# One mask pass instead of two, penalties and signs as steps of the order, a second output buffer, and a new order

## Chip, core, metric

The kernel runs on one core of one Trainium2 chip. The metric is the time of one execution in microseconds (us), the median of three runs. The engines are TensorE (PE, matrix products), VectorE (DVE), ScalarE (ACT), GpSimd (POOL) and SyncE (SP, which here issues the transfers).

## What is computed

Local attention with a few global keys, followed by one dense feed-forward layer. With 4 batches, 8 heads, 768 positions, head size 64, `n_global` 8 and `n_local` 96:

```python
scores = scale * np.matmul(q, k.transpose(0, 1, 3, 2))
keep = is_global | is_local                  # pos < n_global, or 0 <= rel < n_local
bias = -slopes[:, None, None] * dist         # dist: rel, or n_local for a global key that isn't local
scores = np.where(keep, scores + bias, -1e9)
a = softmax(scores); x = np.matmul(a, v)     # 3072 rows of 512
h = x @ w_in                                 # 512 x 2048
sp = np.maximum(h, 0.0) + np.log1p(np.exp(-np.abs(h)))
out = (h * erf(sp)) @ w_out                  # 2048 x 512
```

`q`, `k`, `v` are float32; `w_in` and `w_out` reach the kernel as float64.

## The kernel before

**Tiles.** The 3072 rows are 24 tiles of 128 (six to a batch). A tile's queries meet 256 columns: 120 keys of the tile before, 8 global keys, 128 keys of its own. Two tiles make a unit of 256 rows for the feed-forward part, whose 2048 inner columns are two groups of 1024, each in two halves of 512. Matrix products of the feed-forward part are made in float16 with each operand split into a high and a low half, three products for one.

**Order.** All work of the fast path is a list of steps, `ORDER`, written out as a table. Each word is a step's name, its numbers and, where the engine can be chosen, a letter: `a` ScalarE, `v` VectorE, `p` POOL. `run_fast` calls the steps in that order, and every engine executes its own instructions in the order in which they were recorded. Since one helper records everything, nearly all instructions have the line L195. The names that matter here:

- `Wd`, `Rd`: a transfer of weights. `w_in` comes in eight blocks of 1 MB (`w_in_raw`, into the tile `wo`, four buffers, each used again once its block is done), `w_out` in sixteen chunks of 512 KB (`wo_load`, twelve in tiles named `raw_wo` and four in `wo`).
- The turn from float64 to float32, on the two 32-bit words of each number, in place: `Wi`/`Ri` scales the high word as a float32 (`conv_i`), `Wa`/`Ra` shifts the low word right (`conv_a`; on ScalarE it moves 16-bit halves instead), `Wc`/`Rc` puts the sign into the upper half of the low word (`conv_c`), `Wb`/`Rb` joins the two (`conv_b`). The words stand 8 bytes apart from one element to the next.
- `Wq`, `Wr`, `Wm`, `Wp` and the same with R: a gram product, its maximum, a sum over partitions, and power-of-two scales; then `Wh`/`Rh` and `Wl`/`Rl` make the high and the low float16 half.
- `vd`, `vq`, `vm`, `vp`: the same scales for `v`. `ld` loads a tile of k, q or v; `TK`, `K`, `KC`, `KF` turn k and copy it into the key buffer `kT`, `TQ` and `Qc` do q.
- `S` scores (PE), `E` adds the penalty `pen` and takes the minimum (a custom DVE instruction), `X` exp (ACT), `eh`, `el`, `et` (`eP` for the first tiles) the float16 halves of e and their transpose, `V` the product with v, `x`, `xh`, `xl`, `xt` the attention output.
- `h` up projection (PE) and `H` its copy out of PSUM; `t`, `l`, `i`, `G` tanh, logs, exp and gelu on ScalarE; `P`, `Q`, `c`, `C` products; `g`, `j` the float16 halves; `d` down projection (PE, tile `o`); `O` the scaled output tile (`osb`) and `o` its store.

**Setup.** `setup` reads the two counts, builds a flag that chooses the fast path, issues the first transfers and calls `fast_masks`. That function runs a chain of DVE instructions on a buffer (in `wi_lo`) twice: in the first pass for the first tile of a batch, in the second for the others. After the first pass ScalarE writes two of three column blocks of the penalty for each of 8 heads, 16 instructions; after the second POOL writes the third, 8 instructions. All of it stands ahead of the branch to the fast path on these engines.

Of the kernel before, what the change touches and what calls it, by code (L numbers as in the profile page):

```python
# [74 lines left out]
vh1a Wa3v Wc3 X1,2,1 S2,0 eh1,0,0a ld3,0 Wm2 eh1,0,1a X1,2,0 Ra0a Wb3 V0,2 Wh1a el1,0,1 E2,0,1 vl1 Wp2 Rd5 Wd4 Wq3 va1
Wi4a eP1,2,0 Wr3a x0 eh1,2,0a Wl1 Ri5p Wa4v E2,0,0 X2,0,0 Rc2 Rd3 Wc4 Wd5 Wb4 X2,0,1 el1,0,0 vq1,0,6 Rd1 eP1,2,1
eh1,2,1a Ri4p el1,2,0 Wh2v Ra5a el1,2,1 Wm3 Wi5a vd1,1,6 Wq4 ld2,2 Wl2 S2,2 Wr4a xP0 Wp3 V1,0 Rd6 Wh3a eh2,0,1v V1,2
TK3 Rc0 E2,2,1 eh2,0,0v Ra1a x1 xh0a Wa5a Wl3 el2,0,1p K3a xP1 va2 Wd7 xl0v xh1v X2,2,1 Ra4a Wm4 Wp4 Rc5 xl1v ld3,1
Ri1v Ri3a Wc5 et2,0,1 Rc4 vh2p Ri6p h0,0 Wd6 Rb2 Rc1 Ra6a E2,2,0 Wi7a Rb1 Ra3v Wb5 el2,0,0v Rb0 TQ3 Qc3a ld4,0 Wa7v
h0,1 Wc7 H0,0a Wb7 X2,2,0 eh2,2,1a Rd7 Wh4a Wq5 S3,0 vq1,1,6 Ri7p et2,0,0 Rd12 Wl4 el2,2,1v Rb4 Rd13 Rc3 Wi6a Rc6  # L80
H0,1v h0,2 Wr5v Wa6a Wm5 vl2 et2,2,1 Rb3 eh2,2,0a Wc6 E3,0,1 Ra7a h0,3 E3,0,0 Wp5 TK4 Rq0 vd1,2,6 Ri13v Wb6 Rd14 Wh5a
Rb5 Rc7 Rr0a X3,0,1 Rb6 S3,2 el2,2,0p H0,2a Wl5 Ri12p eh3,0,1v V2,0 vq1,2,6 Wq6 Wq7 el3,0,1p Rd15 E3,2,0 et2,2,0 Ri15p
X3,0,0 Wr6v Rd8 Ra13a X3,2,0 ld3,2 E3,2,1 Wr7a X3,2,1 Rb7 Ri14a Rd10 et3,0,1 Rc13 h1,0 Wm6 Rd9 Ri8p Ra15a K4a Ra12v
Rb13 Ra14v eh3,0,0a Wp6 V2,2 Wm7 x2 Ra8v Wh6p xh2a Wl6 vh3a H1,0a Ri10a Wp7 Wh7a ld4,1 eh3,2,0a Ra10v Rm0 H0,3a Rq1
Rd11 vl3 Rr1a el3,0,0v Rp0 Rc12 vd1,3,6 Rc15 Ri9a Rc10 Rb12 Rc8 Rb10 ld4,2 h1,1 TQ4 Rc14 Ra9a et3,0,0 Rb15 Rc9 Qc4a
h1,2 t0,0 Rb14 vq1,3,6 xl2p ld5,0 S4,0 Ri11a Rq3 TK5 Rb9 ld5,1 Ra11a Rm1 Rr3a va3 Wl7 Rm3 Rh1a eh3,2,1v ld6,0 Rh2a Rb8
el3,2,0p Rp1 H1,1a Rc11 Rh0v Rb11 Rq2 Rl1 K5a et3,2,0 Rh3a Rp3 vd1,4,6 Rr2a H1,2a E4,0,0 vh4a Rl0 t0,1 Rm2 el3,2,1p
Rp2 E4,0,1 t1,0 vq1,4,6 S4,2 Rh11a et3,2,1 Rh10v vl4 Rh8p V3,0 V3,2 Rl10 Rh4p h1,3 xt2 Rl8 TQ5 x3 Rl4 xh3v X4,0,0 l0,0
Rl2 Rh13p eh4,0,0a X4,0,1 xl3v vd1,5,6 Rl11 Rh6p Qc5a vq1,5,6 Rh5p Rh9p E4,2,0 el4,0,0v i0,0 Rh7v E4,2,1 eh4,0,1a xt3
ld6,1 H1,3v Rl6 vm1 el4,0,1v X4,2,1 Rl5 Rl13 G0,0 vd2,0,6 Rl9 X4,2,0 Rl7 h2,0 h2,1 P0,0v vp1 et4,0,0 H2,0a et4,0,1  # L90
eh4,2,0v l0,1 S5,0 Rh12p Q0,0p TK6 G0,1 eh4,2,1v E5,0,0 va4 h2,2 X5,0,0 el4,2,0p et4,2,0 c0,0 E5,0,1 H2,1v Rl12 C0,0
ld7,0 H2,2a g0,0v S5,2 el4,2,1p K6a X5,0,1 h2,3 V4,0 j0,0 E5,2,1 Rl3 TQ6 ld5,2 i0,1 eh5,0,0v l1,0 P0,1v X5,2,1 h3,0
vh5p el5,0,0p et4,2,1 Qc6v eh5,0,1v E5,2,0 i1,0 va5 H2,3v vq2,0,6 d0,0 d0,1 el5,0,1p d0,2 t2,0 Rh14p t1,1 Q0,1v vl5
et5,0,0 KC1,0p G1,0 c0,1 C0,1 h3,1 S6,0 et5,0,1 eh5,2,1a V4,2 E6,0,0 X5,2,0 x4 vd2,1,6 el5,2,1p E6,0,1 ld7,1 d0,3 V5,0
# [1100 lines left out]
```

## Time and profile before

| | |
|---|---|
| median of three runs | 723.23 us (722.84 to 723.86) |
| the profiled execution | 723.82 us; its span, first to last instruction, 722.0 us |
| TensorE busy, mean granted clock | 660.6 us (91%), 0.969 |
| VectorE, ScalarE, POOL busy | 615.2 us, 629.9 us, 233.7 us |

The profile is one execution on the core. Busy time of an engine is a mean over stages with different limits, so a stage's own window tells more than the share of the span. A matmul's end is modelled.

### The profile page before, as it was taken

What the parts mean: (1) busy time and instruction counts of PE and PEld (TensorE: products, weight loads), DVE (VectorE), ACT (ScalarE), POOL (GpSimd) and SP (SyncE); (2) the same over time, 40 slices, a digit from 0 to 9 for tenths busy, and PEclk for the clock granted to TensorE, in tenths of its full rate; (3) what the DMA queues carried; (4) which work ended last, traced back from release to release, by engine and by line L of the source; (5) the groups of instructions that cost most, each with busy time, mean ns of one, the idle gap of its engine ahead of it and who ended that gap; (6) DMA issues with size and microseconds to landing.
All of it is one profiled execution on the core that took longest, in us unless ns stands there. A gap on an engine that the chain in (4) does not pass through costs nothing.

```text
span 722.0 us, 14148 instructions
## 1 busy us (share of the span) xinstructions
PE 660.6 (91%) x5384; PEld 458.9 (64%) x5384; DVE 615.2 (85%) x1141; ACT 629.9 (87%) x1001; POOL 233.7 (32%) x174
## 2 busy tenths in 40 slices
PE   2864768889999999999999999999999999999995
PEld 1553657666675677666766766666776766667552
DVE  3899998899999978998878898999958789867682
ACT  4577778999999999899999999789899999998970
POOL 2031121356342244123642136121533421624200
PEclk9987987799999999999999999999999999999998
DMA  8675986545656655556436565356454454230000
GB/s 264 187 234 171 277 253 112 122 90 117 132 136 115 133 103 118 120 94 110 103 85 129 96 132 116 64 85 127 95 104 114 92 104 88 40 63 30 1 31 34
DMA packets 207553, 83.40 MB, mean 116 GB/s; under 512 B 192988, under 2 KB 192988, under 8 KB 207476
## 3 DMA queue, kind: packets, MB, share of 16 engines
q1 hardware_dynamic: 207476, 82.41, 51.6%
q8 instruction: 44, 0.72, 0.4%
q14 instruction: 33, 0.27, 0.1%
HBM read 41.96 MB, written 6.29 MB: 67 GB/s over the span
## 4 chain that ended last, share of the span: by engine, by line
PE 75%; DVE 16%; ACT 4%; issue 2%; DMA 2%; POOL 1%; POOLq 0%; SPq 0%; DVEq 0%; ACTq 0%
PE h L195 30%; PE o L195 30%; PE s L195 7%; PE po L195 4%; DVE wo L195 3%; DVE e L195 2%; PE kTp L195 1%; PE qTp L195 1%; DVE C L195 1%; DVE raw_wo L195 1%; DVE g L195 1%; DVE wi_lo L195 1%; DVE w L195 1%; DMA kraw<-in_k 1%; ACT L195 1%
## 5 line engine op out<-in xcount | busy, mean ns | idle before, releaser
L195 PE MATMUL h<-xT,wi_hi 128*128 128x256 f16 x1536 | 260.3, 275 | 5.0 <-DVE ex_wi L195 1.6
L195 PE MATMUL o<-wo,g 128*128 128x512 f16 x1152 | 262.7, 379 | 0.1
L195 PE MATMUL h<-xT,wi_lo 128*128 128x256 f16 x768 | 211.2, 275 | 0.0
L195 PEld LDWEIGHTS <-g 128*128 128x128 f16 x1152 | 110.2, 98 | 123.7 <-issue 5.9
L195 PEld LDWEIGHTS <-wi_hi 128*128 128x128 f16 x1536 | 149.4, 99 | 33.1 <-issue 5.4
L195 ACT ACT_TABLE_LOAD x100 | 128.3, 1283 | 1.8
L195 POOL TENSOR_TENSOR w<-e,w 128x512 f16<-128x512 f32 x44 | 63.8, 1451 | 146.8 <-DVE w L195 86.7
L195 ACT ACTIVATE e<-e,mn 128x256 f32<-128x256 f32 x192 | 95.3, 498 | 14.6 <-DVE mn L195 14.2
L195 PEld LDWEIGHTS <-wi_lo 128*128 128x128 f16 x768 | 75.8, 99 | 11.3 <-issue 1.8
L195 DVE SCALAR_TENSOR_TENSOR C<-A,B 128x1024 f32<-128x1024 f32 x48 | 64.6, 1346 | 10.6 <-POOL B L195 10.3
L195 DVE SCALAR_TENSOR_TENSOR g<-C,gs,g 128x1024 f16<-128x1024 f32 x48 | 65.2, 1358 | 8.5 <-POOL g L195 8.0
L195 PE MATMUL s<-kT,qT 64*128 64x256 f32 x384 | 63.2, 437 | 6.0 <-DVE mn L195 3.6
L195 DVE CUSTOM_DVE_ANT_0 e<-s,pen 128x256 f32<-128x256 f32 x160 | 60.5, 418 | 9.4 <-PE s L195 7.6
L195 POOL TENSOR_SCALAR g<-C,gs 128x1024 f16<-128x1024 f32 x24 | 33.3, 1387 | 107.3 <-DVE C L195 81.5
L195 DVE SCALAR_TENSOR_TENSOR C<-C,H 128x1024 f32<-128x1024 f32 x48 | 62.1, 1294 | 0.6
L195 ACT ACTIVATE B<-A 128x1024 f32<-128x1024 f32 x48 | 50.8, 1057 | 5.7 <-DVE C L195 2.9
L195 ACT ACTIVATE A<-A,halves 128x1024 f32<-128x1024 f32 x48 | 54.8, 1142 | 0.2
L195 POOL TENSOR_TENSOR B<-C,B 128x1024 f32<-128x1024 f32 x17 | 41.6, 2447 | 38.7 <-DVE A L195 30.2
L195 PEld LDWEIGHTS s<-kT,qT 64*128 64x128 f32 x384 | 37.3, 202 | 23.4 <-issue 11.8
L195 ACT ACTIVATE C<-A 128x1024 f32<-128x1024 f32 x48 | 50.4, 1053 | 1.0 <-DVE g L195 0.6
L195 ACT ACTIVATE B<-B 128x1024 f32<-128x1024 f32 x48 | 50.2, 1050 | 0.3
L195 ACT ACTIVATE A<-H 128x1024 f32<-128x1024 f32 x48 | 50.0, 1050 | 0.2
(153 smaller groups left out, 974.5 us busy)
## 6 DMA issues: line engine op xcount, KB each, us to landing
wo<-in_moe_w_in SPq DMA_DIRECT2D x8, 1024.0 KB, 9.2
raw_wo<-in_moe_w_out SPq DMA_DIRECT2D x12, 512.0 KB, 6.8
out<-osb SPq DMA_DIRECT2D x24, 256.0 KB, 2.8
qraw<-in_q SPq DMA_DIRECT2D x23, 256.0 KB, 3.6
kraw<-in_k SPq DMA_DIRECT2D x23, 256.0 KB, 3.3
vraw<-in_v SPq DMA_DIRECT2D x23, 256.0 KB, 3.8
va<-vb SPq DMA_DIRECT2D x20, 240.0 KB, 3.6
vm<-in_v SPq DMA_DIRECT2D x18, 256.0 KB, 5.9
```

Source lines behind the costliest of these rows:

```text
L195: i = getattr(self.engine, name)(*a, **k)
```

## The change

What it does:

1. `fast_masks` runs one chain for both kinds of tile and leaves three column blocks (`pd`) side by side: block 0 for the previous keys of a batch's first tile, block 1 for those of the others, block 2 for a tile's own. The global columns get their two forms by three small instructions.
2. The penalty of one head is one instruction of 128x384, a step `pn` of the order with an engine letter. Eight such steps replace the 24 instructions of setup: four on POOL, three on DVE, one on ScalarE.
3. The sign step is a copy of the high word into a float16 (after `conv_i` the number is so small that only its sign is left), with an engine letter. Of 24, ScalarE has 17 (6 `Wc`, 11 `Rc`), POOL 6 (2 and 4), DVE 1.
4. Setup's flag takes fewer DVE instructions; POOL's clearing of the global v rows comes after the mask work.
5. The very last output tile has a buffer of its own (tag `x`), and `osb` is kept for each tile.
6. `ORDER` is another permutation of the same steps, with other letters. Over the whole list, 53 of the float16 copies of e are on ScalarE (41 before), 52 of 88 differences `el` on POOL (44), 46 copies `H` on ScalarE (53).

```diff
-Wi0a TK0 vd0,1,3 K0a TQ0 Qc0a KC0,0p S0,0 E0,0,1 ld1,1 ld1,0 Wa0v Wd1 X0,0,1 TK1 Wc0 vd0,0,3 vd0,2,3 eP0,0,1 K1a
+TK0 K0a Wi0v pn3p pn5v pn6v vd0,1,3 pn2p vq0,1,3 TQ0 Wa0v Qc0a KC0,0p vd0,2,3 pn1p Wc0p ld0,2 S0,0 vd0,0,3 ld1,0
...
-d23,7 O11,0a o11,0 O11,1a o11,1
+d23,0 d23,1 c23,1 d23,2 C23,1 d23,3 g23,1v j23,1 d23,4 d23,5 d23,6 d23,7 O11,0a o11,0 O11,1v o11,1
...
-    def conv_c(self, r):
-
-        s = r.bitcast(I16).rearrange("p a (b w) -> p a b w", w=4)[:, :, :, 1]
-        self.nc.vector.tensor_scalar(s, self.words(r)[1], 0.0, -32768.0, op0=ALU.is_lt, op1=ALU.mult)
+    def conv_c(self, r, e):
+        s = r.bitcast(F16).rearrange("p a (b w) -> p a b w", w=4)[:, :, :, 1]
+        if e == "a":
+            self.nc.scalar.copy(s, self.words(r)[1])
+        else:
+            (self.nc.vector if e == "v" else self.nc.gpsimd).tensor_copy(s, self.words(r)[1])
...
-        for c in range(2):
-            act, pd = mk[:, 2], mk[:, 3]
...
-            for h in range(H):
-                s = -8.0 * SLOPES[h]
-                if c == 0:
-                    nc.scalar.activation(self.pen[:, h, 0], pd[:, 0:P], AF.Copy, scale=s)
-                    nc.scalar.activation(self.pen[:, h, 2], pd[:, P:], AF.Copy, scale=s)
-                else:
-                    nc.gpsimd.tensor_scalar(self.pen[:, h, 1], pd[:, 0:P], s, 1.0, op0=ALU.mult, op1=ALU.mult)
+        nc.gpsimd.memset(pd[:, 0, 0:PREV], big)
...
+        v = nc.vector
+        v.tensor_scalar(act, rel, nl, None, op0=ALU.is_lt)
+        v.scalar_tensor_tensor(act, rel, 0.0, act, op0=ALU.is_ge, op1=ALU.mult)
+        v.tensor_scalar(gl, jg, ng, None, op0=ALU.is_lt)
+        v.tensor_scalar(act[:, g], act[:, g], -1.0, 1.0, op0=ALU.mult, op1=ALU.add)
+        v.tensor_tensor(act[:, g], act[:, g], gl, op=ALU.mult)
+        v.tensor_tensor(rel, act, rel, op=ALU.mult)
+        v.tensor_scalar(rel[:, g], act[:, g], nl, None, op0=ALU.mult)
+        v.tensor_scalar(act, act, -big, big, op0=ALU.mult, op1=ALU.add)
+        two = lambda z: z.rearrange("p (k w) -> p k w", k=2)
+        v.tensor_tensor(pd[:, 1:3], two(rel), two(act), op=ALU.add)
+        v.tensor_copy(pd[:, 0, g], pd[:, 1, g])
+        v.tensor_scalar(gb, gl, -big, big, op0=ALU.mult, op1=ALU.add)
+        v.scalar_tensor_tensor(pd[:, 1, g], gl, nl, gb, op0=ALU.mult, op1=ALU.add)
+        self.pd = pd
+
+    def penalty(self, h, z):
+        s, o = -8.0 * SLOPES[h], self.pen[:, h]
+        if z == "a":
+            self.nc.scalar.activation(o, self.pd, AF.Copy, scale=s)
+        elif z == "v":
+            self.nc.vector.tensor_scalar(o, self.pd, s, None, op0=ALU.mult)
+        else:
+            self.nc.gpsimd.tensor_scalar(o, self.pd, s, 1.0, op0=ALU.mult, op1=ALU.mult)
...
-        o = self.xp.tile([P, DM], F32, tag="osb", name=f"osb_{u}_{t}")
+        tag = "x" if u == B * NT // UT - 1 and t else "osb"
+        o = self.xp.tile([P, DM], F32, tag=tag, name=f"osb_{u}_{t}")
```

The table's rows say little to a reader, so here is where the instructions stand. First DVE behind the branch to the fast path, before the change: `e` and `mn` are a custom instruction (printed as ISA) that makes a masked tile and its minimum, `wo` is the first block of `w_in`, shifted and joined.

```order
L195 ISA e_0_1_216,mn_205<-s_0_1_211,pen 128x256
L195 ISA mn_205 128x1
L195 TENSOR_SCALAR wo<-wo 128x1024 x2
L195 ISA e_0_0_244,mn_205<-s_0_0_210,pen 128x256
L195 ISA mn_205 128x1
L195 ISA e_0_0_244,mn_205<-s_0_0_210,pen 128x256
L195 ISA mn_205 128x1
L195 SCALAR_TENSOR_TENSOR wo<-wo 128x1024
```

Both minima of the first head pair stand ahead of the joining there. The same place on DVE after the change:

```order
L195 TENSOR_SCALAR wo<-wo 128x1024
L195 TENSOR_SCALAR pen<-wi_lo 128x384 x2
L195 TENSOR_SCALAR wo<-wo 128x1024
L195 SCALAR_TENSOR_TENSOR wo<-wo 128x1024
L195 TENSOR_SCALAR pen<-wi_lo 128x384
L195 ISA e_0_1_209,mn_177<-s_0_1_189,pen 128x256
L195 ISA mn_177 128x1
```

The scaling of the first block, two penalties, the shift, the joining and a third penalty now stand ahead of the first minimum; the sign step between shift and joining is gone from DVE.

POOL at the start, before: `pen` are the penalties, `kT` the key buffer (a clearing, then two copies).

```order
L654 TENSOR_SCALAR pen<-wi_lo 128x128 x8
L1156 TENSOR_LOAD flag
L1157 COMPARE_AND_BRANCH
L195 MEMSET kT 128x4x120
L195 TENSOR_SCALAR kT<-kT 128x4x2x8
L195 TENSOR_SCALAR kT<-kT 128x4x8
L195 TENSOR_SCALAR vb_336<-wo,s_v_326 128x8x64
```

All eight penalties, and the branch, are ahead of the key buffer there. POOL at the start after the change:

```order
L195 MEMSET kT 128x4x120
L195 TENSOR_SCALAR pen<-wi_lo 128x384 x2
L195 TENSOR_SCALAR kT<-kT 128x4x2x8
L195 TENSOR_SCALAR pen<-wi_lo 128x384
L195 CAST wo<-wo 128x1024
L195 TENSOR_SCALAR pen<-wi_lo 128x384
L195 TENSOR_SCALAR kT<-kT 128x4x8
L195 TENSOR_SCALAR raw_wo_202<-raw_wo_202 128x512
```

Two of four larger penalties stand ahead of the copy of the keys where eight small ones stood, and the sign of the first block (CAST of `wo`) between the third and the fourth.

Third, DVE in the stage in which the chunks of `w_out` are turned, before: of the rows on `raw_wo`, the TENSOR_SCALAR ones are shifts and signs, the SCALAR_TENSOR_TENSOR ones join.

```order
L195 TENSOR_SCALAR raw_wo_420<-raw_wo_420 128x512
L195 TENSOR_SCALAR wo<-wo 128x1024
L195 TENSOR_SCALAR raw_wo_466<-raw_wo_466 128x512
L195 SCALAR_TENSOR_TENSOR raw_wo_427<-raw_wo_427 128x512
L195 TENSOR_SCALAR raw_wo_420<-raw_wo_420 128x512
L195 ISA e_2_0_784,mn_473<-s_2_0_624,pen 128x256
L195 ISA mn_473 128x1
L195 ISA e_2_0_784,mn_473<-s_2_0_624,pen 128x256
L195 ISA mn_473 128x1
L195 SCALAR_TENSOR_TENSOR raw_wo_420<-raw_wo_420 128x512
L195 TENSOR_SCALAR raw_wo_427<-raw_wo_427 128x512
```

Shifts, signs and joinings of three chunks alternate there. The same stage on DVE after the change (`wi_lo` is a low half of `w_in`, `vb` the v of a tile):

```order
L195 SCALAR_TENSOR_TENSOR wi_lo<-wo,swi,wi_hi 128x4x256
L195 SCALAR_TENSOR_TENSOR raw_wo_202<-raw_wo_202 128x512
L195 SCALAR_TENSOR_TENSOR raw_wo_676<-raw_wo_676 128x512
L195 SCALAR_TENSOR_TENSOR vb_687<-vraw_2_659,s_v_298,vb_687 128x8x64
L195 SCALAR_TENSOR_TENSOR raw_wo_387<-raw_wo_387 128x512
L195 TENSOR_SCALAR wo<-wo 128x1024
L195 SCALAR_TENSOR_TENSOR raw_wo_473<-raw_wo_473 128x512
L195 TENSOR_SCALAR wo<-wo 128x1024
```

On DVE the joinings of four chunks now follow one another, without a sign between them. The signs (CAST of `raw_wo` and of `wo`) stand in this part of ScalarE's queue, where `e` are exps, `gr_wi` a gram maximum, `vm` a square of v and `H` a copy out of PSUM:

```order
L195 ACTIVATE e_2_1_590,sm_476<-e_2_1_590,mn_475 128x256 x2
L195 CAST raw_wo_262<-raw_wo_262 128x512
L195 CAST wo<-wo 128x1024
L195 ACTIVATE raw_wo_473<-raw_wo_473 128x512
L195 ACTIVATE raw_wo_202<-raw_wo_202 128x512
L195 CAST raw_wo_202<-raw_wo_202 128x512 x2
L195 ACTIVATE gr_wi_757,a_wi_808<-gr_wi_757 128x256
L195 ACTIVATE vm_1_385,a_v_374<-vm_1_385 128x512
L195 CAST raw_wo_473<-raw_wo_473 128x512
L195 ACTIVATE H_0_791<-h_1_766,hs_301 128x512
```

Five signs came into these ten rows, among ScalarE's own scalings of chunks.

## Rows read from the trace of the kernel before

**Rows 1.** The page, part 2: busy tenths of TensorE and VectorE in 40 slices
```profile
PE   2864768889999999999999999999999999999995
...
DVE  3899998899999978998878898999958789867682
```

**Rows 2.** Windows: busy us (instructions) of each engine, granted clock, DMA share
```profile
160.00:300.00 140.00, 139.89 (x1161) 94.21 (x1159) 132.18 (x237) 134.84 (x224) 56.52 (x38) 1.00 0.58 119
...
0.00:20.00 20.00, 5.62 (x22) 3.62 (x22) 7.71 (x36) 8.87 (x25) 4.83 (x22) 1.00 0.89 263
20.00:160.00 140.00, 102.74 (x855) 82.19 (x854) 131.04 (x317) 108.47 (x207) 35.16 (x31) 0.85 0.71 183
...
153.70:713.45 559.75, 557.94 (x4583) 378.75 (x4583) 482.60 (x803) 516.04 (x778) 195.79 (x123) 1.00 0.47 95
```

**Rows 3.** Waits of DVE, 20 to 160 us: total, times, longest
```profile
DVE x L195 <- PE po L195: 2.1, 1, 2.1
```

**Rows 4.** The chain that ended last: start, us, what
```profile
160.28 3.89 PE o L195 x18
```

**Rows 5.** Groups by form, DVE, 0 to 160 us: busy us, mean ns, idle before
```profile
L195 DVE TENSOR_SCALAR wo<-wo 128x1024 int16<-128x1024 f32 x8 | 11.0, 1369 | 0.3
...
L195 DVE TENSOR_SCALAR raw_wo<-raw_wo 128x512 int16<-128x512 f32 x12 | 9.3, 811 | 0.0
...
L195 DVE TENSOR_SCALAR wo<-wo 128x512 int16<-128x512 f32 x4 | 3.1, 782 | 0.0
```

**Rows 6.** Timeline 0 to 40 us: start, us, engine, instruction, [idle before]
```profile
2.12 0.58 SPq L269 DMA_DIRECT2D wo<-in_q  x1
...
11.40 1.10 ACT L195 ACTIVATE wo<-wo 128x1024 f32<-128x1024 f32 x1
11.53 0.43 DVE L641 TENSOR_TENSOR wi_lo<-wi_lo 128x256 f32<-128x256 f32 x1 [2.11 <-ACT pen L652]
...
13.11 2.42 POOL L654 TENSOR_SCALAR pen<-wi_lo 128x128 bf16<-128x128 f32 x8 [10.82 <-DVE wi_lo L645]
...
16.34 2.08 PE L195 MATMUL s<-kT,qT 64*128 64x256 f32 x8 [2.20 <-POOL kT L195]
...
18.58 0.42 DVE L195 CUSTOM_DVE_ANT_1 e<-s,pen 128x256 f32<-128x256 f32 x1 [5.57 <-PE s L195]
```

**Rows 7.** Groups by form, DVE, whole span
```profile
L195 DVE TENSOR_SCALAR hs<-iwi,s_v 128x8 f32<-128x8 f32 x3 | 4.5, 1499 | 0.1
...
L195 DVE TENSOR_SCALAR hs<-iwi,s_v 128x1 f32<-128x1 f32 x8 | 1.7, 214 | 0.3
...
L644 DVE TENSOR_SCALAR wi_lo<-wi_lo 128x256 f32<-128x256 f32 x2 | 0.6, 294 | 0.1
```

**Rows 8.** Groups by form, POOL, whole span
```profile
L654 POOL TENSOR_SCALAR pen<-wi_lo 128x128 bf16<-128x128 f32 x8 | 2.2, 297 | 11.0 <-DVE wi_lo L645 10.8
L195 POOL TENSOR_SCALAR wo<-wo 128x1024 f32<-128x1024 f32 x1 | 1.8, 1779 | 4.4 <-DMA wo<-in_moe_w_in 4.4
...
L195 POOL TENSOR_SCALAR wi_hi<-wo,swi 128x1024 f16<-128x1024 f32 x1 | 1.2, 1170 | 2.9 <-DVE iwi L195 2.9
```

**Rows 9.** Groups by form, ACT, whole span
```profile
L195 ACT ACTIVATE raw_wo<-raw_wo 128x512 int16<-128x512 uint16 x9 | 12.2, 1357 | 0.0
...
L195 ACT ACTIVATE wo<-wo 128x1024 int16<-128x1024 uint16 x3 | 7.5, 2510 | 0.0
...
L195 ACT ACTIVATE wi_hi<-wo,swi 128x1024 f16<-128x1024 f32 x6 | 7.4, 1239 | 4.8 <-DVE swi L195 4.8
...
L195 ACT ACTIVATE wo<-wo 128x1024 f32<-128x1024 f32 x5 | 5.8, 1158 | 1.5 <-DMA wo<-in_moe_w_in 1.5
...
L195 ACT ACTIVATE raw_wo<-raw_wo 128x512 f32<-128x512 f32 x3 | 2.2, 722 | 0.0
```

**Rows 10.** Timeline 705 to 723 us
```profile
713.47 0.69 ACT L195 ACTIVATE osb<-o,gs 128x512 f32<-128x512 f32 x1 [11.52 <-PE o L195]
...
716.63 0.69 ACT L195 ACTIVATE osb<-o,gs 128x512 f32<-128x512 f32 x1 [2.47 <-DMA out<-osb]
```

More of the change, by code (lines that the diff above doesn't have):

```diff
@@ L75 @@
[L75 to L94, printed above, removed]
@@ new lines @@
+eh4,2,1v P0,0v et4,0,0 H1,3a E5,0,1 X4,2,0 l0,1 el4,2,1p eh4,2,0v E5,0,0 va4 Q0,0v et4,2,1 h2,1 vh4a TK6 H2,0a
+el4,2,0v S5,2 vl4 G0,1 Rh12p H2,1a c0,0 vd2,0,6 et4,2,0 Rl9 t1,0 X5,0,0 ld5,2 h2,2 h2,3 V4,0 C0,0 Rl12 K6a eh5,0,0a
+ld7,0 V4,2 g0,0v X5,0,1 i0,1 TQ6 eh5,0,1a Rh13v H2,2v E5,2,1 j0,0 el5,0,0p et5,0,0 h3,0 el5,0,1p l1,0 Qc6v H2,3v P0,1v
+E5,2,0 vh5a d0,0 X5,2,1 vl5 KC1,0p d0,1 Q0,1v G1,0 h3,1 Rl13 d0,2 t2,0 va5 c0,1 S6,0 t1,1 eh5,2,1a ld7,1 X5,2,0 x4
+C0,1 E6,0,0 et5,0,1 d0,3 i1,0 H3,0v TQ7 X6,0,0 el5,2,1p V5,0 E6,0,1 xh4a g0,1p eh5,2,0v S6,2 ld6,2 el5,2,0v P1,0v
@@ new lines @@
+et5,2,1 h3,3 Qc7a H3,1a TK7 X6,0,1 j0,1 ld8,1 d0,4 eh6,0,0a l1,1 E6,2,0 KC1,1p Q1,0v K7v X6,2,0 Rh14a xl4p c1,0
+et5,2,0 h3,2 d0,5 C1,0 xt4 vq2,0,6 i1,1 Rl14 V5,2 eh6,2,0a x5 el6,0,0p E6,2,1 et6,0,0 g1,0v vd2,1,6 l2,0 TQ8 d0,6 xh5v
+eh6,0,1a j1,0 H3,2v d0,7 G1,1 vq2,1,6 xl5v vh6p S7,0 d1,0 d1,1 el6,2,0p et6,2,0 xt5 vl6 G2,0 P1,1v Rh15v ld8,0
+el6,0,1p E7,0,1 E7,0,0 t2,1 H3,3v Rl15 X6,2,1 Q1,1p c1,1 C1,1 et6,0,1 i2,0 eh6,2,1a d1,2 g1,1v l2,1 ld9,1 d1,3 S7,2
+h4,2 X7,0,1 i2,1 h4,0 t3,0 vd2,2,6 j1,1 d1,4 P2,0v d1,5 G2,1 Qc8v d1,6 el6,2,1v Q2,0v va6 eh7,0,1v vq2,2,6 c2,0 d1,7
@@ new lines @@
+C15,0 eh19,2,1a g15,0p S20,0 H16,3a P15,1p E20,0,0 el19,2,1v X19,2,0 h17,0 ld21,1 E20,0,1 Q15,1p ld21,0 l16,0 d14,3
+eh19,2,0v xh18a h17,2 H17,0a c15,1 TQ21 X20,0,0 j15,0 d14,4 C15,1 S20,2 X20,0,1 d14,5 el19,2,0p Qc21a V19,0 g15,1p
+h17,1 E20,2,0 TK21 ld20,2 xl18v et19,2,1 et19,2,0 d14,6 V19,2 X20,2,0 xt18 G16,0 d14,7 K21a vh20a eh20,0,0a H17,1a
+ld22,1 j15,1 t16,1 el20,0,0p d15,0 H17,2v i16,0 x19 xh19v xl19v d15,1 vl20 o6,1 E20,2,1 l16,1 d15,2 P16,0v S21,0
+et20,0,0 eh20,0,1a i16,1 xt19 d15,3 el20,0,1v eh20,2,0a d15,4 E21,0,0 X20,2,1 Q16,0p G16,1 el20,2,0v P16,1p h17,3
@@ L184 @@
+d21,7 h23,3 O10,0a h23,2 P22,1p o10,0 Q22,1v j22,0 c22,1 G23,0 O10,1a H23,2a d22,0 d22,1 H23,3v o10,1 C22,1 P23,0v
+g22,1v j22,1 t23,1 l23,1 Q23,0v c23,0 i23,1 d22,2 G23,1 d22,3 C23,0 d22,4 d22,5 g23,0v d22,6 j23,0 P23,1v Q23,1v d22,7
+d23,0 d23,1 c23,1 d23,2 C23,1 d23,3 g23,1v j23,1 d23,4 d23,5 d23,6 d23,7 O11,0a o11,0 O11,1v o11,1
 """.split()]
@@ L234, in setup @@
         lo, hi = f2[:, 0, :], f2[:, 1, :]
-        neg = cp.tile([P, 2], F32, name="nneg")
-        nc.vector.tensor_scalar(neg, lo, 0.0, None, op0=ALU.is_lt)
         hi2 = cp.tile([P, 2], F32, name="nhi2")
-        nc.vector.tensor_tensor(hi2, hi, neg, op=ALU.add)
+        nc.vector.scalar_tensor_tensor(hi2, lo, 0.0, hi, op0=ALU.is_lt, op1=ALU.add)
         self.nval = cp.tile([P, 2], F32, name="nval")
@@ L617, in fast_masks @@
         self.pen = cp.tile([P, H, 3, P], BF16, name="pen")
-        mk = self.wi_lo.rearrange("p c f -> p (c f)").bitcast(F32)[:, 0 : 4 * WIN].rearrange("p (a w) -> p a w", a=4)
-        rel, jg, gl = mk[:, 0], mk[:, 1, 0:NGL], mk[:, 1, NGL : 2 * NGL]
+        big = BIG / SLOPES[-1]
+        mk = self.wi_lo.rearrange("p c f -> p (c f)").bitcast(F32)
+        rel, act = mk[:, 0:WIN], mk[:, WIN : 2 * WIN]
+        pd = mk[:, 2 * WIN : 2 * WIN + 3 * P].rearrange("p (k w) -> p k w", k=3)
+        jg, gl, gb = (mk[:, 4 * WIN + k * NGL : 4 * WIN + (k + 1) * NGL] for k in range(3))
         it = lambda o, n, base: nc.gpsimd.iota(
@@ L974, in o_part @@
             self.nc.vector.tensor_scalar(o, po, s, None, op0=ALU.mult)
-        self.osb = o
+        self.osb[u, t] = o
     def o_store(self, u, t):
         r = u * U + t * P
-        self.nc.sync.dma_start(self.out[r : r + P, :], self.osb)
+        self.nc.sync.dma_start(self.out[r : r + P, :], self.osb.pop((u, t)))
     def gen_batch(self, b):
@@ L1060, in branch @@
             self.cb, self.hb = (CB, HB) if fast else (1, 2)
-            for n in ("pt", "vs", "qT", "us", "vm", "a_v", "gr", "a1", "hs", "h_done", "raw_wo", "raws", "tp", "cs", "va", "vb", "xT", "hp", "H", "A", "B", "C", "g", "pos"):
+            for n in ("pt", "vs", "qT", "us", "vm", "a_v", "gr", "a1", "hs", "h_done", "raw_wo", "raws", "tp", "cs", "va", "vb", "xT", "hp", "H", "A", "B", "C", "g", "pos", "osb"):
                 setattr(self, n, {})
@@ L1090, in run_fast @@
         do = dict(
-            Wd=self.w_in_raw,
+            pn=self.penalty, Wd=self.w_in_raw,
             Wi=lambda n, z: conv(lambda r: self.conv_i(r, z), self.wi_raw(n)),
             Wa=lambda n, z: conv(lambda r: self.conv_a(r, z), self.wi_raw(n)),
-            Wc=lambda n: conv(self.conv_c, self.wi_raw(n)),
+            Wc=lambda n, z: conv(lambda r: self.conv_c(r, z), self.wi_raw(n)),
             Wb=lambda n: conv(self.conv_b, self.wi_raw(n)),
```

221 lines of the change are left out of this document (104 added, 117 removed).

## The prediction

> **What bounds the kernel now.** I read the page first, then the windows by stage. The page shows where TensorE lacks work: its row of tenths starts with nine digits from 2 to 8 and is then 9 up to the last slice, while the row of VectorE (DVE) is 8 and 9 from the second slice on [rows 1]. The windows show it in numbers. From 20 to 160 us DVE is busy 131.04 of 140 us, ScalarE (ACT) 108.47, and TensorE 102.74 at a granted clock of 0.85; from 153.70 to 713.45 us TensorE is busy 557.94 of 559.75 at 1.00 [rows 2]. So the program has two parts. In the first the weights are turned from float64 into two float16 halves and the first tiles of attention are made; DVE sets its pace. DVE's longest wait between 20 and 160 us is one of 2.1 us [rows 3]; five shorter ones follow it in that view. It waits for hardly anybody. The second part begins about the first down projection, at 160.28 us [rows 4], and TensorE sets its pace to the end. TensorE's work is the same in both kernels (the order holds the same matmul steps), so the end moves by as much as the first down projection moves, plus what the last output saves, plus stalls that a new order may put into the second part.
>
> **What is removed from DVE.** The sign step runs 24 times on DVE: 8 instructions of 11.0 us, 12 of 9.3 and 4 of 3.1, 23.4 us, all before 160 us [rows 5]. In the new order one of the 24 stays on DVE as a cast (at most the 0.78 of the old form, and not below zero). The second mask pass goes: in the timeline its end releases POOL's penalties at 13.11, and DVE is idle 2.11 us inside it because ScalarE's penalties still read the buffer [rows 6]; its eight instructions are the same as in the first pass, 2.5 us of work.
>
> **What is added to DVE before the first down projection.** Three penalties of 128x384, a form that the trace does not show. The nearest row is the 128x256 multiply-add at 294 ns [rows 7]; by its size one is 0.44, all three 1.3. Bounds for one are 0.29 and 0.88 (three times that of 128x128 on POOL, 297 ns, [rows 8]), so 0.9 to 2.6. Four more shifts of the low words (5 to 6 and 5 to 8 by the letters, 0.4 to 0.7 each, estimated as a half of the sign step) give 2.0, and one more maximum of a gram of w_in and two of w_out about 1.8. The attention steps that change engines before that point nearly cancel (two fewer float16 copies of e, two more copies of q, one product, one v scaling): +0.3. Sum: 23.4 + 2.5 - 0.8 - 1.3 - 2.0 - 1.8 - 0.3, near 20 us; durations overlap by some 50 ns at each start, so I take **18 us less DVE**.
>
> **What ScalarE pays.** It gets 6 signs of 128x1024 and 11 of 128x512, f32 in and f16 out, at a step of 8 bytes. The trace has no such form. Two rows lie on either side: the float32 scaling in place at the same step takes 1158 and 722 ns, and the 16-bit shift in place, also at that step, 2510 and 1357 [rows 9]. By the first the signs cost 6 x 1.158 + 11 x 0.722 = 14.9 us, by the second 6 x 2.510 + 11 x 1.357 = 30.0. I take the first: the input is 32 bits wide as there, and the writing of float16 from a stepped float32 (the high half of w_in) also took only 1239 [rows 9]. ScalarE sheds 16 penalties (their starts stand 0.2 apart, 3.2 us), four 16-bit shifts (2.5 + 3 x 1.36 = 6.6), two halves of w_in (2.5) and two scalings of w_in (2.3), and gets two scalings of w_out (1.4) and one penalty of 128x384 (0.3 to 0.9). With the maxima that leave it, that is about 0 to +2: **ScalarE's work up to the first down projection stays near the 117.3 us of the trace** (8.87 and 108.47, [rows 2]).
>
> [...]
>
> **The start.** Before, the first scores wait for POOL's copies of k, which stand behind eight penalties of 2.42 us in POOL's queue; DVE idles 5.57 us and its first mask-and-minimum begins at 18.58 [rows 6]. In the new order DVE reaches the branch when one mask pass is done (about 8.5 us), and then waits for w_in's first block, which had landed by 11.40, when ScalarE used it [rows 6]. Behind that wait stand two penalties, the shift, the sign on POOL (1.17 to 1.78, [rows 8]) and the combining step, so the scores' first minimum comes at about 17, and the first block of w_in is ready five to six us sooner. DVE has thus done about 12 us of work by 20 us, where it had done 7.71 [rows 2].
>
> **First down projection.** DVE's work up to 160 us was 7.71 + 131.04 = 138.75 [rows 2]; less 18 it is 120.7. With 12 done at 20 us, 108.7 remain. Were DVE as dense as before (0.936), they would take 116 us and the projection would come at 136. But ScalarE now has as much to do (117 less some 9), and each waits for the other on every block of weights. From 160 to 300 us the two are busy 0.94 and 0.96 together [rows 2], so two full engines are possible; I choose 0.86, since here a chain of eight blocks with four buffers runs through both. 108.7/0.86 = 126, so it comes at 146: **14 us sooner**. Bounds: 0.936 gives 24 sooner, 0.76 gives 3.
>
> **The last output.** The second tile of the last output waits 2.47 us for the store of the first, from one buffer, and starts at 716.63, 3.16 after the first [rows 10]. With a buffer of its own and on DVE it starts with the first at 713.47; its store queues behind the first store's issue (0.58 for as many bytes, [rows 6]). **2.5 us saved**; 0 if the store's issue were the limit, 3.2 at most.
>
> **Stalls later.** From 160 to 300 us ScalarE has 5.2 us of 140 free [rows 2]. In that part the new order gives it about 4 us more than before (five more float16 copies of e, one more log step, fewer copies out of PSUM), and over the whole rest about 1. I charge 1.5 (0 to 6).
>
> **Sum.** 723.82 (the profiled execution, span 722.0 and 1.8 around it) - 14 - 2.5 + 1.5 = 708.8. The median is 0.6 below the profiled execution, so **708 us**. Under 0.2% (1.4 us) a change of this kernel can't be told from none.
>
> **The rivals.**
> 1. *Forecast*, 703 to 713 us: chance 0.60. A density over 0.90 would give less than 703: 0.06.
> 2. *The sign copy costs ScalarE what its 16-bit shift costs.* Then it has 15 us more, some 132 up to the first down projection; at 0.86 behind the first 20 us that is 163, no gain, and only the last output and the start remain: 718 to 722. For it: the 16-bit row at the same step. Against: the float32 input, and that the shift also converts integers. 0.13. [...]
> 3. *POOL takes from DVE what the change gives.* POOL has about 11 us more before the first down projection (two more scalings and halves of w_in each, six signs). The row that shows the two colliding is a product of 128x8 on DVE, 1499 ns on average in three, where one of 128x1 takes 214 [rows 7]. If each of those 11 us held DVE up, 3 of the 14 were left: 718 to 719. Against: DVE was 0.94 busy beside POOL anyway, and much of DVE's work there reads PSUM. 0.06. [...]
> 4. *The weights don't come sooner.* The DMA engines are busy 0.71 of 20 to 160 us [rows 2]; the same bytes in 126 us need 0.79, and 0.89 was reached in the first 20. If the queue adds half of the saving back: 715 to 716. 0.08.
> 5. *Slower.* ScalarE passes work that it could not do into the second part. There it has 43.7 us free of 559.75, but only 5.2 up to 300 us, so a backlog of B us stalls TensorE by up to B. It decides from B = 16.5 on, where 14 + 2.5 are eaten: 725 and more. For it: 11 signs at the end of the weights, just before the first tanh and log groups. Against: they are 0.7 us each, and ScalarE had 31 us of idle time between 20 and 160. 0.07.
>
> The range must leave out no more than 0.2: from 702 to 719 it holds case 1, case 4, most of case 3 and the near half of the 0.06 on one side and of case 2 on the other. Faster: cases 1, 3, 4, the 0.06 and nearly all of 2, 0.90. Same: the end of case 2 and between 2 and 5, 0.03. Slower: 0.07.
>
> **What would show it.** Right: no 16-bit multiply on DVE; ScalarE's casts at 1.1 to 1.3 us for 1024 and about 0.7 for 512; the first minimum at about 17 us; the first down projection near 146; both engines at 0.85 or so from 20 us to there; two output tiles starting together at the end. Wrong: casts over 2 us, DVE instructions that stretch while POOL is busy, TensorE idle by more than 3 us after the first down projection.

## The result, and the profile after

| | before | after |
|---|---|---|
| median | 723.55 us (722.84 to 724.44, 4 runs) | 714.29 us (713.80 to 714.79, 4 runs) |
| profiled execution, span | 723.82 us, 722.0 us | 713.80 us, 711.6 us |

The ratio is 0.987, 95% interval 0.985 to 0.989: the change saves 9.3 us. Forecast were 708 us and a range of 702 to 719; the time lies in the range, and the gain is 9 us where 15 were expected.

The page of the changed kernel, part 2, has TensorE's tenths a little higher at the start than in [rows 1], and VectorE no longer at 9 there:

```profile
PE   3668777999999999999999999999999999999996
...
DVE  5788788999999979898897799888977999795894
```

The windows of the changed kernel, with the columns of [rows 2]. The first `o` matmul starts at 153.8 and the last output at 705.04, so the window of 551.24 us is the second part:

```profile
0.00:20.00 20.00, 7.82 (x36) 5.97 (x36) 10.69 (x36) 9.93 (x20) 9.12 (x21) 1.00 0.91 270
20.00:160.00 140.00, 109.49 (x906) 87.28 (x906) 120.50 (x305) 126.03 (x210) 44.64 (x36) 0.79 0.74 189
160.00:300.00 140.00, 140.00 (x1175) 96.00 (x1173) 131.51 (x234) 136.25 (x233) 68.35 (x41) 1.00 0.60 119
...
0.00:153.80 153.80, 111.11 (x900) 89.25 (x901) 124.99 (x329) 129.83 (x221) 51.73 (x56) 0.81 0.76 199
153.80:705.04 551.24, 550.87 (x4484) 372.79 (x4483) 478.48 (x775) 510.38 (x775) 213.81 (x129) 1.00 0.47 95
```

Read against the window of before: from 20 to 160 us VectorE fell from 131.04 to 120.50, but ScalarE rose from 108.47 to 126.03. I read this as one engine that set the pace before and two that share it now; runs 2, 3, 5 and 10 test it. The waits of VectorE from 20 to 160 us say the same (total, times, longest); in [rows 3] the longest was one of 2.1 us for TensorE:

```profile
DVE wo L195 <- ACT wo L195: 6.5, 4, 2.7
DVE e L195 <- PE s L195: 3.5, 2, 2.3
DVE raw_wo L195 <- ACT raw_wo L195: 1.9, 1, 1.9
DVE raw_wo L195 <- POOL raw_wo L195: 1.2, 1, 1.2
```

The rows for `wo` and `raw_wo` are VectorE's joinings, waiting for signs. The groups by form name the reason (busy us, mean ns, idle before); they answer to [rows 5] and stand beside the shift of [rows 9]:

```profile
L195 ACT CAST wo<-wo 128x1024 f16<-128x1024 f32 x6 | 15.8, 2640 | 1.7 <-issue 1.7
L195 ACT CAST raw_wo<-raw_wo 128x512 f16<-128x512 f32 x8 | 11.2, 1484 | 0.0
L195 ACT ACTIVATE raw_wo<-raw_wo 128x512 int16<-128x512 uint16 x7 | 10.3, 1476 | 0.0
L195 POOL CAST raw_wo<-raw_wo 128x512 f16<-128x512 f32 x4 | 6.9, 1731 | 11.5 <-ACT raw_wo L195 9.2 <-DVE raw_wo L195 2.3
L195 POOL CAST wo<-wo 128x1024 f16<-128x1024 f32 x2 | 4.9, 2473 | 4.5 <-ACT wo L195 3.6 <-DVE wo L195 0.9
...
L195 ACT CAST wo<-wo 128x512 f16<-128x512 f32 x3 | 4.3, 1428 | 0.0
```

A sign copy costs ScalarE 2640 and 1484 ns, the price of the 16-bit shift in the same trace (2598 and 1476) and not that of the float32 scaling (1206 and 762). The 17 took 31.3 us (15.8 + 11.2 + 4.3) where 14.9 were reckoned.

The start, to set beside [rows 6]:

```profile
9.19 0.93 DVE L195 TENSOR_SCALAR wo<-wo 128x1024 f32<-128x1024 f32 x1 [0.79 <-DMA wo<-in_moe_w_in]
...
11.67 2.47 POOL L195 CAST wo<-wo 128x1024 f16<-128x1024 f32 x1 [0.88 <-DVE wo L195]
...
14.17 1.23 DVE L195 SCALAR_TENSOR_TENSOR wo<-wo 128x1024 int32<-128x1024 int32 x1 [2.57 <-POOL wo L195]
...
15.90 0.41 DVE L195 CUSTOM_DVE_ANT_1 e<-s,pen 128x256 f32<-128x256 f32 x1
```

The first minimum comes at 15.90 (18.58 before), although VectorE waits 2.57 us for POOL's copy of 2.47. And the end, beside [rows 10]:

```profile
705.04 0.69 ACT L195 ACTIVATE osb<-o,gs 128x512 f32<-128x512 f32 x1 [11.51 <-PE o L195]
705.68 0.75 DVE L195 TENSOR_SCALAR osb<-o,gs 128x512 f32<-128x512 f32 x1 [5.02 <-PE o L195]
705.75 1.56 SPq L195 DMA_DIRECT2D out<-osb  x2
```

The second tile starts 0.64 behind the first instead of 3.16, and both stores go out together. From 705.04 to the end of the span are 6.6 us; before, from 713.47, 8.5.

So the 10.4 us between the spans of these two executions split into three: 6.3 because the first down projection starts at 153.8 instead of 160.1, 2.1 because the second part is 551.2 long instead of 553.4, and 1.9 at the end.

### The profile page after: what moved, and what is told of

The parts are those of the page before. It is cut to its first block, busy times and chain, and to the rows that moved or that the text cites. A ratio compares the mean times of both kernels' runs of the same rounds, so it can differ in the third digit from the quotient of the medians.

```text
span 711.6 us, 14143 instructions
## 1 busy us (share of the span) xinstructions
PE 662.6 (93%) x5384; PEld 462.1 (65%) x5384; DVE 604.2 (85%) x1104; ACT 640.9 (90%) x995; POOL 265.5 (37%) x184
## 5 line engine op out<-in xcount | busy, mean ns | idle before, releaser
L195 POOL TENSOR_TENSOR w<-e,w 128x512 f16<-128x512 f32 x52 | 74.3, 1432 | 133.9 <-ACT w L195 68.8
L195 PE MATMUL s<-kT,qT 64*128 64x256 f32 x384 | 65.3, 448 | 8.7 <-DVE mn L195 4.8
L195 DVE SCALAR_TENSOR_TENSOR g<-C,gs,g 128x1024 f16<-128x1024 f32 x48 | 68.2, 1423 | 2.8 <-POOL g L195 1.3
L195 POOL TENSOR_TENSOR B<-C,B 128x1024 f32<-128x1024 f32 x19 | 50.6, 2662 | 40.8 <-DVE A L195 40.3
L195 POOL TENSOR_TENSOR A<-A,B 128x1024 f32<-128x1024 f32 x15 | 37.5, 2497 | 53.7 <-ACT C L195 43.9
L195 POOL TENSOR_SCALAR g<-C,gs 128x1024 f16<-128x1024 f32 x21 | 26.9, 1282 | 80.4 <-DVE C L195 44.0
L195 PEld LDWEIGHTS s<-kT,qT 64*128 64x128 f32 x384 | 39.4, 208 | 25.6 <-issue 13.4
```

The source lines that it names most:

```text
L195: i = getattr(self.engine, name)(*a, **k)
```

## The experiments

The theory after the result: the sign copies' price on ScalarE ate the rest of the forecast gain, because ScalarE became a second bound beside VectorE. The rivals: something else holds the first part (weights, TensorE's granted clock, which is 0.50 from 40 to 50 us, or POOL taking from VectorE), or the order and the start make the gain and the moved signs nothing. All ratios are to the kernel before, timed beside each kernel.

| kernel | us | ratio (95%) | first `o` matmul |
|---|---|---|---|
| after | 714.29 | 0.987 (0.985 to 0.989) | 153.8 |
| 1 tail alone | 721.63 | 0.997 (0.996 to 0.998) | 160.5 |
| 2 ScalarE's signs 32 bits wide | 706.12 | 0.976 (0.975 to 0.978) | 145.8 |
| 3 signs on VectorE | 721.46 | 0.996 (0.995 to 0.998) | 162.2 |
| 4 signs alone, old order | 736.55 | 1.018 (1.017 to 1.020) | 172.2 |
| 5 ScalarE's shifts 32 bits wide | 709.43 | 0.981 (0.978 to 0.983) | 149.8 |
| 6 as 5, four signs to POOL | 710.69 | 0.982 (0.980 to 0.985) | 151.6 |
| 8 masks alone | 721.82 | 0.999 (0.997 to 1.000) | 157.7 |
| 9 as 5, first sign on VectorE | 710.78 | 0.981 (0.980 to 0.983) | 150.4 |
| 10 before, shifts 32 bits wide | 723.58 | 1.000 (0.999 to 1.001) | 157.4 |
| 11 after, scores done twice | 715.40 | 0.988 (0.987 to 0.990) | 157.0 |

The first `o` is that of one execution; in run 10 it moves by 2.7 us while the median stays (the profiled execution took 721.47 us, 2.1 less than the median), so it is evidence only for larger steps. Run 7 was executed once, and only the durations of its copies are used.

**1. The tail alone, in the kernel before.**

```diff
-        o = self.xp.tile([P, DM], F32, tag="osb", name=f"osb_{u}_{t}")
+        tag = "x" if u == B * NT // UT - 1 and t else "osb"
+        o = self.xp.tile([P, DM], F32, tag=tag, name=f"osb_{u}_{t}")
...
-d23,7 O11,0a o11,0 O11,1a o11,1
+d23,7 O11,0a o11,0 O11,1v o11,1
```

> The kernel before, with one part of the change alone: the last output tile has a buffer of its own and is scaled on VectorE. In the trace of the changed kernel 6.6 us pass from the end of the last down projection to the end of the span, 8.5 before. Theory: the tail is worth these 1.9 us whatever stands ahead of it, so 721.6 us (ratio 0.997). Rival: the two stores' issue or landing limits the end and the 1.9 us come from something else; then 723.5 (ratio 1.000).

721.63 us: 2.2 us less (1.3 to 3.2). The tail gives its gain by itself.

**2. The price of the sign copy.**

```diff
-            self.nc.scalar.copy(s, self.words(r)[1])
+            self.nc.scalar.copy(self.words(r)[0], self.words(r)[1])
```

> The changed kernel, but ScalarE's 17 sign copies write a whole 32-bit word in place of its upper half (the weights of those blocks get wrong magnitudes; the instructions, their order and their waits stay). By the scaling rows each then costs 1.16 and 0.72 us in place of 2.64 and 1.48, 16 us less on ScalarE. Theory (price of the 16-bit copy): the missing part of the gain comes back, 708 us (706 to 711, ratio to before 0.976 to 0.983). Rival (the feed of weights or the half clock of TensorE holds the first part): 713.5 to 715, ratio 0.986 to 0.989.

706.12 us. The copies took what the scaling takes (groups by form, 0 to 160 us), and the window up to the first `o` matmul shows VectorE dense again, 115.61 of 125.80:

```profile
L195 ACT COPY wo<-wo 128x1024 f32<-128x1024 f32 x6 | 6.8, 1132 | 2.5 <-issue 1.5 <-DVE wo L195 1.1
L195 ACT COPY raw_wo<-raw_wo 128x512 f32<-128x512 f32 x8 | 5.2, 678 | 0.0
L195 ACT COPY wo<-wo 128x512 f32<-128x512 f32 x3 | 2.1, 699 | 0.0
```

```profile
20.00:145.80 125.80, 98.65 (x868) 81.10 (x868) 115.61 (x294) 106.08 (x203) 43.14 (x35) 0.85 0.78 201
```

The copies take 14.1 us in place of 31.3 on ScalarE. The ratio falls by 0.987 - 0.976 = 0.011, which is 8 us, and the first down projection comes at 145.8. The price theory holds, and the weights come soon enough at that pace.

**3. All signs back on VectorE, in the new order.**

```diff
-        s = r.bitcast(F16).rearrange("p a (b w) -> p a b w", w=4)[:, :, :, 1]
...
+        s = r.bitcast(I16).rearrange("p a (b w) -> p a b w", w=4)[:, :, :, 1]
+        self.nc.vector.tensor_scalar(s, self.words(r)[1], 0.0, -32768.0, op0=ALU.is_lt, op1=ALU.mult)
```

> The changed kernel with all 24 signs on VectorE again in the old form of 16-bit multiply, everything else as changed. VectorE gets 23.4 - 0.7 us back, ScalarE loses 31, POOL 12. Theory (moving the signs is where the gain comes from): the first part is VectorE's again, 719 to 723 us, of the gain only the last output and the start are left. Rival (the new order and the start make the gain, the sign move costs ScalarE what it gives VectorE): 713 to 716.

721.46 us. Order, start, masks and tail together are worth about 2 us; moving the signs is worth 0.996 - 0.987, some 7 us, even at the double price. The rival falls. The windows from 20 us to the first `o`, of the changed kernel and of this run, show what the move does to the two engines in one and the same order:

```profile
20.00:153.80 133.80, 103.29 (x865) 83.27 (x865) 114.30 (x294) 119.90 (x201) 42.61 (x35) 0.78 0.74 189
20.00:162.20 142.20, 106.19 (x868) 85.17 (x867) 132.35 (x316) 93.98 (x184) 34.87 (x30) 0.77 0.68 178
```

With the signs moved, VectorE has 114.30 us in place of 132.35 and ScalarE 119.90 in place of 93.98. Before the change ScalarE had 108.57 from 20 us to its first `o` (117.44 in all, 8.87 of it up to 20 us), so the new order takes 14.6 us off ScalarE before any sign comes to it.

**4. The sign copies alone, in the old order** (letters as after).

```diff
-Wc0 ... Wc1 ... Wc2 ... Rc0 ... Rc11
+Wc0p ... Wc1a ... Wc2a ... Rc0a ... Rc11a
```

> The kernel before with the sign copies alone: the same blocks and chunks on the same engines as in the changed kernel, in the old order, with the old masks and tail. ScalarE gets 31 us in the first 160, of which it had 43 idle, and its copies stand where VectorE's stood. Theory (price): ScalarE becomes the bound in an order not made for it, 720 to 728. Rival (the move gives its gain in any order): 714 to 717.

736.55 us, 13 us slower, beyond what either expected. VectorE's waits up to 175 us:

```profile
DVE wo L195 <- ACT wo L195: 15.5, 6, 3.6
DVE raw_wo L195 <- ACT raw_wo L195: 8.6, 2, 6.9
```

The window from 20 us to the first `o`:

```profile
20.00:172.20 152.20, 104.33 (x857) 82.82 (x856) 112.61 (x294) 134.12 (x224) 42.86 (x38) 0.76 0.67 168
```

ScalarE is busy 134.12 of the 152.20 us (0.88), and VectorE waits 24 us for its work on the weights, nearly all of it at joinings. ScalarE pays for the signs here what it pays in the new order: 134.12 - 108.57 = 25.6 us, against 119.90 - 93.98 = 25.9, and it is nearly as dense as there (0.88, against 0.90). What differs is the load under them, the 14.6 us that the new order's letters take off ScalarE. At a density of 0.88 they are worth 16.6 of the 18.4 us by which the first `o` comes later here than in the changed kernel. Whether the place of the copies in ScalarE's queue adds to the loss is not shown. So the signs' gain needs the room that the new order makes on ScalarE, and that order alone (run 3, less the tail) has next to no gain: neither part is the gain by itself.

**5. ScalarE's shift with a 32-bit write.**

```diff
-            self.nc.scalar.activation(h(I16, 0), h(U16, 1), AF.Copy, scale=2.0 ** -13, bias=-0.5 + 2.0 ** -14)
+            self.nc.scalar.activation(self.words(r)[0].bitcast(I32), h(U16, 1), AF.Copy, scale=2.0 ** -13, bias=-0.5 + 2.0 ** -14)
```

> The changed kernel, but ScalarE's ten shifts of the low word (7 of 128x512 at 1476, 2 of 128x1024 at 2598, one of 1469 in a wo tile; 17.0 us) still read the 16-bit half and write the whole 32-bit word as an integer. Result the same. Theory (a 16-bit write at a step of 8 bytes costs double, whatever is read): they cost 0.72 and 1.16, 8.9 us less on ScalarE; 16 us less gave 8.2 us, so 4.4 us: 710 us. Rival (the 16-bit read, or the conversion to an integer, sets the price): 714.3, no change.

709.43 us, faster than both kernels: the shifts take 8.4 us less on ScalarE (17.0 to 8.6), and the ratio falls by 0.0065, which is 4.7 us. The shift reads 16 bits as before and writes 32 (groups by form):

```profile
L195 ACT ACTIVATE raw_wo<-raw_wo 128x512 int32<-128x512 uint16 x7 | 5.3, 760 | 0.0
...
L195 ACT ACTIVATE wo<-wo 128x1024 int32<-128x1024 uint16 x2 | 2.5, 1236 | 0.0
```

**6. As 5, and four signs from ScalarE to POOL.**

```diff
-Rc1a ... Rc4a ... Rc7a ... Rc8a
+Rc1p ... Rc4p ... Rc7p ... Rc8p
```

> As the run with 32-bit shifts, and four of ScalarE's signs of 128x512 (chunks 1, 4, 7, 8) on POOL: ScalarE 5.9 us less, POOL 6.9 more (it is busy 39 of 120 us there). Theory (ScalarE still is one of the two bounds): 2 to 3 us less than that run, 707 to 708. Rival (POOL does them late, or takes the time from VectorE): 710 to 713, that run or worse.

710.69 us, no gain over run 5. ScalarE fell from 102.87 to 97.21 us (20 to 140), but VectorE's joinings of chunks rose from 712 to 842 ns each:

```profile
L195 DVE SCALAR_TENSOR_TENSOR raw_wo<-raw_wo 128x512 int32<-128x512 int32 x12 | 9.8, 842 | 0.0
```

The theory's 2 to 3 us did not come, and the rival's range holds. Up to the first `o` VectorE has the same 329 instructions in both runs, and they keep it busy 128.24 us here and 125.34 in run 5, while ScalarE falls from 122.60 to 118.45: of the 4.2 us that ScalarE is spared, 2.9 come back on VectorE, 1.6 of them in the joinings. That fits the rival's second half (POOL takes the time from VectorE).

**7. What a copy on ScalarE costs, by form.**

```diff
+                for j in (n % 9, (n + 4) % 9):
+                    dst, src = (
+                        (v(scr, F16, 1, 0), i),
+                        (v(scr, F16, 2, 1), i),
...
+                    self.nc.scalar.copy(dst, src)
```

> The changed kernel with two more copies of 128x512 on ScalarE before each of its 11 signs of chunks, into a buffer of a later stage: nine forms that differ in the width and step of what is read and of what is written. Only their own durations count; 22 copies more make the kernel longer. Theory (width and step of the write): 1.4 us for f16 or int16 written 8 bytes apart, whatever is read; about 0.7 for f16 written side by side, for f32 written 8 bytes apart, from 16-bit or 32-bit input. Rival (mixed width or conversion): 16-bit to 16-bit is fast, f32 to f16 slow also side by side.

The timeline of ScalarE, one row for each form. In order, what is read and what is written, with the step in bytes: f32 at 8 to f16 at 8; f16 at 8 to f16 at 2; f32 at 8 to f16 at 4; f16 at 8 to f16 at 8; f32 at 8 to f16 at 2; f32 at 8 to int16 at 8; f32 at 8 to f32 at 8:

```profile
65.26 1.34 ACT L195 CAST scr<-raw_wo 128x512 f16<-128x512 f32 x1
66.63 0.66 ACT L195 COPY scr<-raw_wo 128x512 f16<-128x512 f16 x1
...
74.72 0.86 ACT L195 CAST scr<-raw_wo 128x512 f16<-128x512 f32 x1
75.61 1.37 ACT L195 COPY scr<-raw_wo 128x512 f16<-128x512 f16 x1
...
80.44 0.65 ACT L195 CAST scr<-raw_wo 128x512 f16<-128x512 f32 x1
...
121.00 1.32 ACT L195 CAST scr<-wo 128x512 int16<-128x512 f32 x1
122.35 0.68 ACT L195 COPY scr<-wo 128x512 f32<-128x512 f32 x1
```

Of all 22 copies, every 16-bit write at a step of 8 bytes takes 1.32 to 1.39 us, from 32-bit input and from 16-bit input alike, and everything else 0.64 to 0.86. It is the write.

**8. Masks and penalties alone, at the head of the old order.**

```diff
-Wi0a TK0 vd0,1,3 K0a TQ0 Qc0a KC0,0p S0,0 E0,0,1 ... X0,0,1 TK1 ...
+Wi0a TK0 pn3p pn5v pn6v vd0,1,3 K0a pn2p TQ0 Qc0a KC0,0p pn1p S0,0 pn0p pn7v E0,0,1 ... X0,0,1 pn4a TK1 ...
...
```

> The kernel before with the single mask chain and the eight penalties of 128x384 as steps at the head of the old order (three on VectorE, four on POOL, one on ScalarE), signs and tail as before. By the terms of the prediction VectorE has 2.5 us less of masks, 1.7 more of penalties (0.57 each as measured after), and its first minimum comes up to 2.7 us sooner. Theory (VectorE is dense behind the start, so each microsecond of its work or of a sooner start moves the end by 0.9): 720.5 us, 3 sooner. Rival (the start is not on the path, or the penalties delay the first keys on POOL): 723 to 724.

721.82 us; the interval reaches from no gain to 2.2 us, so the theory's 3 us did not come, and whether there is a gain at all stays open. The first minimum came at 17.19, 1.4 sooner.

**9. As 5, the first block's sign on VectorE** (`Wc0p` to `Wc0v`).

> The run with 32-bit shifts, and the sign of w_in's first block as a copy on VectorE in place of POOL, where it took 2.47 us and VectorE waited 2.57. On VectorE it costs about 1.4 (the 736 of 128x512 for twice as many), in time that it idles. Theory (the start is on VectorE's path): the first minimum 1.1 us sooner, 708.4 us. Rival (later waits take it up): 709.4, the run with 32-bit shifts.

710.78 us; by the ratios the same as run 5. The first minimum came at 14.91 (15.87 in run 5), but VectorE then waits 2.31 us for TensorE before the maximum of w_in's first gram (1.93 in run 5), and the minimum behind that one comes at 22.04 (22.11 in run 5). The rival holds: later waits take it up.

**10. The 32-bit shift in the kernel before** (edit of run 5).

> The kernel before with one edit: ScalarE's 14 shifts of the low word (9 of 1357, 3 of 2510, 2 of 1360; 22.5 us) write a 32-bit word, by the form measured in the changed kernel 0.76 and 1.24: 12.1 us, 10.4 less. Theory (VectorE alone sets the pace of the first part before the change): 722.5 to 723.5, no change beyond 1 us. Rival (ScalarE shares the pace there too): some half of 10 us, 718.

723.58 us, no change. The 14 shifts took 10.8 us in place of 22.4 and nothing followed, so ScalarE had no share in the pace. The same edit is worth 4.7 us after the change and nothing ahead of it.

**11. More work for TensorE at the start.**

```diff
-        for a in range(2):
+        for a in [0, 1] * (2 if i < 3 else 1):
```

> The changed kernel with the score matmuls of the first three tiles done twice (the same result written twice): some 10 us more work for TensorE in the first 50 us, where its granted clock was 0.50 to 0.67 after the change and it was busy 7 of 10. Rival (the half clock is part of what the first part lost): a higher clock there and 1 us or more less, under 713. Theory (TensorE is not what holds the first part): 714 to 716; above 717 the scores' own latency is on the path.

715.40 us, within the two intervals the same as after. The granted clock from 20 to 50 us rose from 0.71 to 0.89 without a gain. The added matmuls delay the scores too, so this run could hide a small gain; that the lower clock is not where the missing microseconds went rests on run 2 as well, which got them back by the price of the copies alone.

## Why the prediction was right, and where it was off

**The bound of before: right.** Run 10 takes 11.6 us from ScalarE and moves nothing; the changed kernel takes 14 from VectorE (138.85 to 124.99 up to the first down projection) and moves the end.

**What VectorE sheds: 14, not 18.** Run 3 splits the sum, as it has the same order with the signs on VectorE. Up to its first `o` VectorE is busy 143.95 us (11.60 up to 20 us, 132.35 behind it), 5.1 more than before, where the terms other than the signs came to 2.9 (1.3 + 2.0 + 1.8 + 0.3 - 2.5). Moving the signs then takes off 19.0 (143.95 - 124.99), though their durations add up to 22.7 (23.4 less one copy of 0.74): neighbouring records overlap, and by more than the 50 ns that were reckoned. So of the 4 us that lack some 2 lie in the other terms (penalties, for one, cost 0.57 each where 0.44 was estimated) and some 2 in the overlap, for which the forecast had taken off 2 and the trace takes off 3.7. The third rival, POOL taking from VectorE, does not explain the lack. Seven float16 copies of e took 824 ns each up to 160 us where run 3, without signs on POOL, has 467, which is 2.5 us; but in run 3 other instructions are longer, five shifts of chunks 789 ns each where the changed kernel has 452, and the durations of all 328 instructions that VectorE has in both up to the first `o` add up to 0.4 us more, no more than that, in the changed kernel. The forecast's point against this rival, that much of VectorE's work there reads PSUM, has a number in the trace of before: the 43 copies of `h` out of PSUM on VectorE took 714 to 751 ns each, at least 23 of them for half of their time or more beside an instruction on POOL.

**The sign copy on ScalarE: the step that failed.** "I take the first: the input is 32 bits wide as there, and the writing of float16 from a stepped float32 [...] also took only 1239." That row writes side by side; run 7 shows that the width of the input does not matter and the step of the 16-bit write does (1.32 to 1.39 us at 8 bytes, 0.64 to 0.75 side by side). The term is 31.3 us, not 14.9. In busy time, in which overlapping records count once, the signs add 25.9 us to ScalarE (run 3 against the changed kernel), and the other terms held: without the signs ScalarE has 103.9 us up to the first down projection (93.98 and 9.93), 13.5 less than before, where the forecast had 13 to 15. So its work there is 129.8, not 117.3. Run 2 puts the lower price back: 706.1 us where 708 was forecast, and the first down projection at 145.8 where 146 was.

**The density: a lucky pair.** In run 2 VectorE had 115.6 us to do behind the first 20, not 108.7, and was 0.92 busy, not 0.86. The two errors cancel. One of the bounds has a wrong sign: at 0.76 the 108.7 us take 143, and the projection comes at 163, some 3 us later than before and not 3 sooner.

**The range: held by luck.** The forecast's own case was 703 to 713 us, and 714.29 lies outside it. The range went up to 719 for the third and fourth rivals (POOL, weights) and half of the second; what came is the second rival's cause with a good half of its effect. Of the signs of being wrong, casts over 2 us came (2640 ns).

**The second rival: its premise was right, its sum was not.** With 15 us more on ScalarE it gave 718 to 722 from a density of 0.86. ScalarE ran at 0.90 (119.90 of 133.80), VectorE at 0.85, so the double price took 8 us back and not all 14. It had a chance of 0.13; the row that agrees in the step and in the width of what is written deserved more.

**The start: first minimum right (17 forecast, 15.90), 12 us done by 20 not** (10.69): POOL's copy of the first block took 2.47 where 1.17 to 1.78 stood, and behind the first minima VectorE waits 1.15 for the gram and 2.27 for scores. Run 9 shows that the first of these was worth nothing in the end.

**The end: 2.5 forecast, 1.9 in the trace, 2.2 in run 1.** The mechanism is as told, but the second tile starts 0.64 behind the first, since it waits for TensorE.

**Later stalls: 1.5 charged, none came.** In the second part TensorE is idle 0.37 us where it was idle 1.81, and it has 24 matmuls less to do there, since more were done ahead of the first down projection (900 against 876); together these are the 2.1 us that the second part is shorter, which the sum had left out. ScalarE's 136.25 of 140 us after 160 did no harm. The backlog rival did not occur.

**The feed of weights: not a limit.** Run 2 starts the first down projection 14 us sooner than before at a DMA share of 0.78.

What stays open: in run 5 VectorE and ScalarE are busy 0.89 and 0.87 of the time from 20 us to the first down projection (115.51 and 112.63 of 129.80), and neither POOL (run 6) nor a faster first block (run 9) brings it nearer. A new order made for the true prices was not tried.
